# Four tiles of x are turned once and kept, the second half's turns and statistics get fixed steps, and the last z tile's PSUM bank is moved

## Chip, core and metric

One kernel runs on one NeuronCore of a Trainium2 chip. Its engines are TensorE (PE, with its weight loads as PEld), VectorE (DVE), ScalarE (ACT), GpSimd (POOL) and SyncE (SP, which here only issues DMAs). The metric is device time in microseconds (us) of one launch. Three runs of the kernel before gave 1761.16, 1761.31 and 1762.13 us; their median, 1761.31 us, is the number that the change is compared with.

## The reference

Everything is float32; S = 2048 rows, D = 512 columns.

```python
xn = layernorm(x)
# A: 32 heads of 128, keys and values: the last 512 rows of the cache
q = xn @ wq                                   # per head 2048 x 128
s = softmax(q @ k.T * 128 ** -0.5) @ v @ wo
# B: gated MLP with mixing along the rows
z = gelu(xn @ w_in)                           # 2048 x 1376
z1, z2 = z[:, :688], layernorm(z[:, 688:])
g = (z1 * (w_sp @ z2 + b_sp[:, None])) @ w_out
out = x + s * silu(g)
```

## The kernel before, in words

Every product of float32 matrices is made of three matmuls on a high and a low half (`mm3`): ACT casts the high half (`copy`), and DVE or POOL subtracts it from the whole (`rest`, line 59) for the low half. The order of all work is written out by hand; each engine runs its own instructions in the order of the program, and a semaphore holds one back until what it needs is done. SP's DMAs are in that order too.

**Start.** The 16 row tiles of x (128 rows each) are normalised and turned. The first eight lie in `sacc`. `flip` turns one by four transposes through the PE into a PSUM bank, and `ln_flip(i)` splits it into the blocks `X[0]`. There are eight PSUM banks: four in the pool `ps_acc` (name `ps_a`, banks 0 to 3) and four in `ps_step` (`ps_3`, banks 4 to 7). A pool gives out the bank that was released longest ago; whoever writes it first waits for its last reader or writer.

**q by fewer products.** For heads after the first two, q is made in a scheme of seven products in place of eight, which needs sums and differences of tiles p and 4 + p (`T1` to `T4`). The kernel before turns tiles 0 to 3 a second time for them: `t_sums(p)` at steps -3 to 0 of the main loop, with `row_sums` (three operations on DVE) behind it.

**Main loop.** `for t in range(T0, T1)` has 512 numbered steps and some before and behind. Step t holds `score(t)` (scores of one 128-row tile of one head: three matmuls, then DVE's maximum `nm`, then ACT's `prob`), some products of `q_products`, `pv` (three matmuls) for step t - 13, and `outp` (three matmuls, then DVE adds the result to `sacc`, line 592) for step t - 18. DVE also transposes `prob` (`turn`, line 541), a DMA through `p_dram` finishes the turn, and `shares` splits it for `pv`: high on ACT (line 560), low on POOL (`pT_l`). A block of four steps (one head and 512 rows) needs `qT` of its own. q of four blocks is made in a round of 16 steps (`LEAD`, `q_span`, `q_events`): step numbers modulo 16 tell what q does. Its low halves `qT_l` are made on DVE at steps 2, 5 and 9 of 16; the one at step 2 is needed by the score at step 4. `score` and `outp` share the four banks of `ps_step`. With one exception in four, a score waits until DVE has read the `outp` of two steps earlier, and every fourth `outp` (steps 1, 5, 9, 13 of 16) waits for DVE's read of the `outp` just one step earlier.

**Second half of x.** `later_x(p)`, for p = 0 to 3, brings tiles 8 + p and 12 + p during steps 30 to 220: load, statistics on DVE (`tile_stats`: BN_STATS and BN_AGGR; `row_stats`: a TENSOR_SCALAR at line 74, then POOL), normalising on ACT (`apply`), a transposition on DVE (`turn_x`, recorded at line 801), a trip through DRAM (`send`, `fetch`), ACT's reordering (`ordered`), sums on POOL (`sums`) and stores for later. A rule sets its steps: an entry at every 2.4 steps on average, so that they fall where they fall in q's round.

**Behind the loop.** Sixteen tiles of z2 follow (`z_product` into a PSUM bank, `z_gelu`: gelu on ACT and BN_STATS on DVE, `z_norm`). Then the pools close and the mixing begins: `products` writes into the banks of a new pool (`pp2`, line 932), the first of them bank 0. The output projection ends the kernel.

Of the kernel before, what the change touches and what calls it, by code (L numbers as in the profile page):

```python
# [8 lines left out]
F32 = mybir.dt.float32  # L9
# [3 lines left out]
OP = mybir.AluOpType  # L13
# [4 lines left out]
P = 128  # L18
S, D = 2048, 512
H, DH, W = 32, 128, 512  # L20
NT = S // P
NC = D // P
# [18 lines left out]
def mixer_kernel(ctx: ExitStack, tc: tile.TileContext, x, wh, w_in, w_sp, b_sp, w_out, out):  # L41
# [8 lines left out]
    nc = tc.nc  # L50
# [10 lines left out]
    late = []  # L61
# [21 lines left out]
    ps_acc = psum.enter_context(tc.tile_pool(name="ps_acc", bufs=4, space=PSUM))  # L83
# [72 lines left out]
    def block():  # L156
        return x8([P, 2, 2, 512])
# [54 lines left out]
    def flip(t, late=False):  # L212
        ps = ps_acc.tile([P, NC, P], F32, name="ps_a") if late else ps_step.tile([P, NC, P], F32, name="ps_3")
        for c in range(NC):
            nc.tensor.transpose(ps[:, c, :], t[:, c * P:(c + 1) * P], ident)
        return ps

    def ln_flip(i, parts=1):
        n, j = divmod(i, 4)
        if j == 0:  # L220
            for h in range(2):
                X[0][h, n] = block()
        if parts == 1:
            ps = flip(sacc[:, i, :])
        else:
            ps = ps_step.tile([P, NC, P], F32, name="ps_3")
        rests, rest_of = [], []
        for h in range(2):
            if parts > 1:
                for c in (2 * h, 2 * h + 1):  # L230
                    nc.tensor.transpose(ps[:, c, :], sacc[:, i, c * P:(c + 1) * P], ident)
            hi, lo = (quarter(X[0][h, n][:, a], j) for a in range(2))
            nc.scalar.copy(hi, ps[:, 2 * h:2 * h + 2])
            rests.append((lo, ps[:, 2 * h:2 * h + 2], hi))
        if n == 1:
            p2, y = ps.rearrange("p c q -> p (c q)"), sacc[:, i, :]
            nc.scalar.copy(y[:, :256], p2[:, :256])
            rest_of.append((y[:, 256:], p2[:, 256:], y[:, :256]))
        if parts > 1:
            return rests  # L240
        for r in rests:
            rest(nc.vector, *r)
        for r in rest_of:
            nc.vector.tensor_tensor(*r, op=OP.subtract)

    TS = ("T2", "T1", "T3", "T4")

    def row_sums(ps, y, o):

        nc.vector.tensor_tensor(o[:, :256], y[:, :256], ps[:, :256], op=OP.subtract)  # L250
        nc.vector.tensor_tensor(o[:, 256:], ps[:, :256], y[:, 256:], op=OP.add)
        nc.vector.tensor_tensor(y[:, :256], ps[:, 256:], o[:, 256:], op=OP.subtract)

    def t_sums(p):
        if p == 0:
            X[0].update((k, block()) for k in TS)
        row_sums(flip(sacc[:, p, :]).rearrange("p c q -> p (c q)"), sacc[:, 4 + p, :], sacc[:, p, :])

    def t_split(p):
        y, o = sacc[:, 4 + p, :], sacc[:, p, :]  # L260
# [38 lines left out]
    def later_x(p):  # L299

        a, b, key = T8 + p, T8 + 4 + p, 100 * (p + 1)
        t, nb = {}, {}

        def row():
            return xq.tile([P, 512], F32, name="rawx")

        def load():
            for i in (a, b):
                t[i] = row()
                nc.sync.dma_start(t[i], x[i * P:(i + 1) * P, :])  # L310

        def row_stats():
            ln_scale(2, key)
            for k, i in enumerate((a, b)):
                mean, r = rx[key + k]
                nb[i] = tmp[key][:, k:k + 1]
                nc.gpsimd.tensor_scalar(nb[i], mean, r, -1.0, op0=OP.mult, op1=OP.mult)

        def apply(i):
            nc.scalar.activation(t[i], t[i], AF.Identity, bias=nb[i], scale=rx[key + (i == b)][1])  # L320

        def turn_x(i):
            src, t["t", i] = t[i], row()
            late.append((nc.vector.transpose, t["t", i].rearrange("p (a c q) -> p a c q", a=4, q=Q),
                         src.rearrange("p (c a q) -> p a c q", a=4, q=Q)))

        def send(i):
            nc.sync.dma_start(x_turn[p][i == b].rearrange("i r a f -> (i r) (a f)"), t["t", i])

        def fetch(i):  # L330
            t["f", i] = row()
            of = x_turn[p][i == b].rearrange("i r a f -> a r i f")
            for g in range(4):
                nc.sync.dma_start(t["f", i][Q * g:Q * g + Q].rearrange("p (i f) -> p i f", i=4), of[g])

        def ordered(i):
            t[i] = row()
            nc.scalar.copy(t[i].rearrange("p (c i q) -> p i c q", i=4, q=Q), t["f", i].rearrange("p (i c q) -> p i c q", i=4, q=Q))

        def quarters():  # L340
            return [t[i][:, 256 * h:256 * h + 256] for i in (a, b) for h in range(2)]

        def part():
            st = t[0, 1] = xq.tile([P, 512], F32R, name="rawx")
            sl = t[b][:, :256]
            nc.scalar.copy(st[:, :256], sl)
            rest(nc.gpsimd, st[:, 256:], sl, st[:, :256])

        def sums(k):
            b11, b21, b12, b22 = quarters()  # L350
            if k == 0:
                u, v = row(), row()
                t.update({"T1": u[:, :256], "T2": u[:, 256:], "T4": v[:, :256], "T3": v[:, 256:]})
            to, x0, x1, op = (("T1", b12, b11, OP.subtract), ("T3", b22, b12, OP.subtract),
                              ("T2", b22, t["T1"], OP.subtract), ("T4", b21, t["T2"], OP.subtract))[k]
            nc.gpsimd.tensor_tensor(t[to], x0, x1, op=op)

        def store(*ks):
            for k in ks:
                if k in ("a", "b"):  # L360
                    send(a if k == "a" else b)
                elif k in WHOLE:
                    src = t[k] if k in TS else quarters()[2 * k[1] + k[0]]
                    nc.sync.dma_start(xd[1, k][:, :, p * P:(p + 1) * P], halves(src))
                else:
                    nc.sync.dma_start(xd[1, k][:, :, :, p * P:(p + 1) * P],
                                      t[k].bitcast(F32).rearrange("p (a c q) -> p a c q", a=2, q=P))

        seq = [load, None, None, lambda: tile_stats(t[a], key, 0), lambda: tile_stats(t[b], key, 1), row_stats,
               lambda: apply(b),  # L370
               lambda: (turn_x(b), apply(a)),
               lambda: turn_x(a),
               None,
               lambda: fetch(b),
               lambda: fetch(a),
               lambda: ordered(b),
               lambda: ordered(a),
               part,
               lambda: sums(0),
               lambda: sums(1),  # L380
               lambda: sums(2),
               lambda: sums(3)]
        stores = {8: ("b",), 9: ("a",), 14: ((1, 1),), 15: ((0, 0), (1, 0)), 16: ((0, 1), "T1"), 17: ("T3",), 18: ("T2",), 19: ("T4",)}
        return [(f, stores.get(n, ())) for n, f in enumerate(seq + [None])], store
# [23 lines left out]
    def z1_out(i, n, ps):  # L408
        z = zs.tile([P, NB], F32, name="z1")
        nc.scalar.copy(z, ps[:, :NB])  # L410
        nc.scalar.dma_start(z1_dram[:, i, n * NB:(n + 1) * NB], z)

    def z1_piece(i, n, between=lambda: None):
        z1_out(i, n, z1_product(i, n, between))
# [186 lines left out]
    def at(t, f, *args):  # L601
        todo.setdefault(t, []).append((f, args))
# [52 lines left out]
                q_events.setdefault(t0 + done + 2, []).append((q_done, g, k))  # L655

    for p in range(4):
        at(-3 + p, t_sums, p)
        at(-2 + p, t_split, p)
    ends = {}  # L660
    ends.setdefault(-2, []).append((keep_x, (0, 1)))
# [7 lines left out]
    ends.setdefault(16 * (NG - 1) - LEAD + 9, []).append((fetch_x, 1, (0, 1)))  # L669
    for k in ((0, 0), (1, 0)):  # L670
        ends.setdefault(NSTEP + 6, []).append((fetch_x, 0, k))
    n, t = 0, 28
    for p in range(4):
        seq, store = later_x(p)
        for k, (f, ks) in enumerate(seq):
            t = max(t + 2, 30 + 12 * n // 5)
            for key in ks:
                at(t, store, key)
            if f:
                at(t, f)  # L680
            n += 1

    load_x(0, 1)
    load_early(0, [(0, 2)])
# [57 lines left out]
    rest(nc.vector, *lowq)  # L742
    z1_out(0, 1, ps)
    z1_out(1, 1, ps1)
    ln_apply(rows[4], 4)
    ln_apply(rows[5], 5)
    z1_piece(2, 0)
    ln_open(6)
    ln_open(7)
    z1_piece(2, 1)  # L750

    FILL = dict(zip((-7, -6, -5, -4, -3, -2, -1, 0, 1, 8),
                    [(i, 1) for i in range(3, T8)] + [(i, 0) for i in range(4, T8)] + [(3, 0)]))
# [237 lines left out]
    for pos, i in enumerate(ZO):  # L991
        if pos > 2 and pos % 2:
            z_split(pos - 2)
        for n in (2, 3):
            z_product(i, n)
            z_gelu(i, n)
        z_norm(pos)
        z_apply(pos - 1)
        if pos == 5:
            for k in ((0, 1), (1, 1)):  # L1000
                fetch_x(0, k)
        t = pos - NT
        if t in (-6, -4, -3):
            prep((-6, -4, -3).index(t), nc.vector)
        step(t)
# [225 lines left out]
```

## Time and profile before

| what | us |
|---|---|
| median of three runs | 1761.31 |
| the profiled execution, its own time | 1761.58 |
| its span, first to last instruction | 1759.7 |
| start, to the first step of the main loop | 0 to 42.6 |
| main loop | 42.6 to about 1364 |
| z2 of 16 tiles, then mixing from | 1487.2 |
| last matmul | 1755 |

The profile's page gives busy times by engine, the chain of work that ended last and the costliest groups. The waits view adds up who waited for whom. The timeline shows instructions in order of time: its columns are start, duration, engine, line, operation, tiles (out<-in), shape, count, and in brackets the idle time before and what ended it. A matmul's duration includes its way through the array; two matmuls in a row overlap, so the cost of one is the distance between the starts.

### The profile page before, as it was taken

What the parts mean: (1) busy time and instruction counts of PE and PEld (TensorE: products, weight loads), DVE (VectorE), ACT (ScalarE), POOL (GpSimd) and SP (SyncE); (2) the same over time, 40 slices, a digit from 0 to 9 for tenths busy, and PEclk for the clock granted to TensorE, in tenths of its full rate; (3) what the DMA queues carried; (4) which work ended last, traced back from release to release, by engine and by line L of the source; (5) the groups of instructions that cost most, each with busy time, mean ns of one, the idle gap of its engine ahead of it and who ended that gap; (6) DMA issues with size and microseconds to landing.
All of it is one profiled execution on the core that took longest, in us unless ns stands there. A gap on an engine that the chain in (4) does not pass through costs nothing.

```text
span 1759.7 us, 28541 instructions
## 1 busy us (share of the span) xinstructions
PE 1753.1 (100%) x8431; PEld 1503.3 (85%) x8431; DVE 1489.9 (85%) x2458; ACT 1185.8 (67%) x2621; POOL 1239.4 (70%) x1171
## 2 busy tenths in 40 slices
PE   9999999999999999999999999999999999999999
PEld 8888888888888887888888888888888899999997
DVE  6789889899899889988888888888888647887875
ACT  5877777777777777777777777777777546543333
POOL 2888998988988989888888888888888411000032
PEclk9999999999999999999999999999999999999999
DMA  6688888988989989788787777877888652655496
GB/s 204 213 237 260 260 250 242 261 240 244 269 246 253 258 235 273 223 255 223 223 228 219 232 225 220 226 218 225 229 224 255 210 192 86 223 189 176 149 259 204
DMA packets 177468, 398.45 MB, mean 226 GB/s; under 512 B 24480, under 2 KB 58528, under 8 KB 158112
## 3 DMA queue, kind: packets, MB, share of 16 engines
q1 hardware_dynamic: 172704, 390.99, 75.7%
q10 hardware_dynamic: 4608, 5.64, 0.9%
q8 instruction: 66, 1.08, 0.3%
q14 instruction: 90, 0.74, 0.1%
HBM read 231.65 MB, written 164.89 MB: 225 GB/s over the span
## 4 chain that ended last, share of the span: by engine, by line
PE 99%; ACT 0%; DVE 0%; issue 0%; POOL 0%; DVEq 0%; POOLq 0%; ACTq 0%
PE ps_a L503 17%; PE ps L65 13%; PE ps L67 13%; PE ps L66 13%; PE ps L932 11%; PE ps_a L570 7%; PE ps_a L569 7%; PE ps_a L568 7%; PE ps_a L66 2%; PE ps_a L67 2%; PE ps_a L65 2%; PE ps_f L66 1%; PE ps_f L67 1%; PE ps_f L65 1%; PE ps_f L932 1%; PE ps_f L1139 0%
## 5 line engine op out<-in xcount | busy, mean ns | idle before, releaser
L59 POOL TENSOR_TENSOR pT_l<-pL,pT_h 128x512 fp32r<-128x512 f32 x507 | 659.2, 1303 | 170.9 <-ACT pT_h L560 162.6
L532 ACT ACTIVATE prob<-ps,nm 128x512 f32<-128x512 f32 x512 | 353.6, 691 | 340.8 <-DVE nm L530 331.8
L592 DVE SCALAR_TENSOR_TENSOR sacc<-ps,sums,sacc 128x512 f32<-128x512 f32 x496 | 369.3, 745 | 115.0 <-PE ps L67 109.4
L503 PE MATMUL ps_a<-x,x 128*128 128x512 f32 x1266 | 365.5, 389 | 0.0
L541 DVE STREAM_TRANSPOSE pL<-prob 128x512 f32<-128x512 f32 x512 | 358.6, 700 | 0.4 <-ACT prob L532 0.4
L530 DVE TENSOR_REDUCE nm<-ps 128x1 f32<-128x512 f32 x512 | 339.9, 664 | 3.0 <-PE ps L67 2.9
L560 ACT CAST pT_h<-pL 128x512 fp32r<-128x512 f32 x512 | 318.5, 622 | 7.3 <-ACT z L410 4.9
L503 PEld LDWEIGHTS ps_a<-x,x 128*128 128x128 f32 x1266 | 237.7, 188 | 49.3 <-issue 0.2
L59 POOL TENSOR_TENSOR wl<-raw,wh 128x512 fp32r<-128x512 f32 x186 | 241.9, 1300 | 11.0 <-ACT wh L145 11.0
L65 PE MATMUL ps<-wh,qT_h 128*128 128x512 f32 x512 | 200.7, 392 | 0.3 <-DVE sacc L592 0.2
L67 PE MATMUL ps<-wh,qT_l 128*128 128x512 f32 x512 | 200.0, 391 | 0.0
L570 PE MATMUL ps_a<-pT_l,wh 128*128 128x512 f32 x512 | 199.6, 390 | 0.0
L65 PE MATMUL ps<-wh,oT_h 128*128 128x512 f32 x512 | 199.4, 390 | 0.0
L66 PE MATMUL ps<-wl,qT_h 128*128 128x512 f32 x512 | 199.4, 389 | 0.0
L66 PE MATMUL ps<-wl,oT_h 128*128 128x512 f32 x512 | 199.4, 389 | 0.0
L568 PE MATMUL ps_a<-pT_h,wh 128*128 128x512 f32 x512 | 199.4, 389 | 0.0
L569 PE MATMUL ps_a<-pT_h,wl 128*128 128x512 f32 x512 | 199.4, 389 | 0.0
L67 PE MATMUL ps<-wh,oT_l 128*128 128x512 f32 x512 | 199.3, 389 | 0.0
L932 PE MATMUL ps<-b,x 128*128 128x344 f32 x1248 | 191.8, 316 | 0.0
L932 PEld LDWEIGHTS ps<-b,x 128*128 128x128 f32 x1248 | 191.5, 188 | 0.0
L59 POOL TENSOR_TENSOR b<-b 128x512 fp32r<-128x512 f32 x2 | 2.5, 1293 | 189.5 <-DMA x<-x 189.5
L59 POOL TENSOR_TENSOR x<-wq,x 128x256 fp32r<-128x256 f32 x177 | 131.6, 744 | 0.0
(212 smaller groups left out, 3047.7 us busy)
## 6 DMA issues: line engine op xcount, KB each, us to landing
p_dram<-pL SPq DMA_DIRECT2D x128, 1024.0 KB, 4.8
pL<-p_dram SPq DMA_DIRECT2D x256, 192.0 KB, 4.1
raw<-wh SPq DMA_DIRECT2D x188, 256.0 KB, 6.3
pL<-p_dram SPq DMA_DIRECT2D x256, 128.0 KB, 4.1
x<-w_sp SPq DMA_DIRECT2D x24, 1024.0 KB, 5.1
pL<-p_dram SPq DMA_DIRECT2D x256, 64.0 KB, 4.0
wq<-wh SPq DMA_DIRECT2D x60, 256.0 KB, 5.7
z_dram<-z ACTq DMA_DIRECT2D x32, 172.0 KB, 3.0
```

The costliest lines, as they stand in the source:

```text
L59: engine.tensor_tensor(lo, whole, hi.bitcast(F32), op=OP.subtract)
L65: nc.tensor.matmul(ps, lh, rh, start=first, stop=False)
L66: nc.tensor.matmul(ps, lh, rl, start=False, stop=False)
L67: nc.tensor.matmul(ps, ll, rh, start=False, stop=last)
L503: nc.tensor.matmul(qps[g, bank], wt["q", g, k][a][:, c * P:(c + 1) * P], X[g * 2 // H][ORDER[k]][:, b, c], start=first, stop=r == 5, skip_ ...
L530: nc.vector.tensor_reduce(nm, ps, axis=AX.X, op=OP.max, negate=True)
L532: nc.scalar.activation(prob[t], ps, AF.Exp, bias=nm, accum_out=sums[b][:, j:j + 1])
L541: nc.vector.transpose(pL[b][:, :, j * P:j * P + P].rearrange("p a (c q) -> p a c q", q=Q), prob.pop(t).rearrange("p (a c q) -> p a c q", a ...
L568: nc.tensor.matmul(pps[b], vh, ph, start=c == 0, stop=False)
L570: nc.tensor.matmul(pps[b], vh, pl, start=False, stop=c == 3)
L592: nc.vector.scalar_tensor_tensor(at, ps, rs, at, op0=OP.mult, op1=OP.add)
L932: nc.tensor.matmul(ps, a, b, start=k != "P4" and c == 0 and m == 0, stop=c == RP - 1 and m == 2, skip_group_check=True)
```

## The change

The four second turns go. `ln_flip(i)` keeps the bank of each turned tile; for tiles 0 to 3, ACT copies it whole into a row buffer (`keep_whole`), and when tile 4 + p is turned, `row_sums` makes all four differences at once, on DVE, at the end of steps -7 to -4 (pushed on `late`). `t_sums` is gone; `t_blocks` only opens the blocks. Tiles 0 and 1 turn into banks of `ps_acc`.

`later_x(p)` has fixed steps, 28 + 48 p + `WHEN_X[k]`, and its stores 28 + 48 p + `STORE_X[key]`. As 48 is three rounds, each entry falls on the same step of q's round for all p. Both `apply` now stand at one step.

Ahead of the last z product, a bank of `ps_acc` is taken and a memset of one column is written to it, so that the product gets the next bank.

```diff
+    def keep_whole(i):
+        p2, whole[i] = whole[i], xq.tile([P, 512], F32, name="rawx")
+        nc.scalar.copy(whole[i], p2)
...
         if parts == 1:
-            ps = flip(sacc[:, i, :])
+            ps = flip(sacc[:, i, :], i == 1)
         else:
-            ps = ps_step.tile([P, NC, P], F32, name="ps_3")
+            ps = ps_acc.tile([P, NC, P], F32, name="ps_a")
...
         if n == 1:
-            p2, y = ps.rearrange("p c q -> p (c q)"), sacc[:, i, :]
+            y = sacc[:, i, :]
             nc.scalar.copy(y[:, :256], p2[:, :256])
-            rest_of.append((y[:, 256:], p2[:, 256:], y[:, :256]))
+            late.append((row_sums, p2, y, sacc[:, i - 4, :], whole[i - 4]))
+        whole[i] = p2
...
-    def row_sums(ps, y, o):
-
-        nc.vector.tensor_tensor(o[:, :256], y[:, :256], ps[:, :256], op=OP.subtract)
-        nc.vector.tensor_tensor(o[:, 256:], ps[:, :256], y[:, 256:], op=OP.add)
-        nc.vector.tensor_tensor(y[:, :256], ps[:, 256:], o[:, 256:], op=OP.subtract)
-
-    def t_sums(p):
-        if p == 0:
-            X[0].update((k, block()) for k in TS)
-        row_sums(flip(sacc[:, p, :]).rearrange("p c q -> p (c q)"), sacc[:, 4 + p, :], sacc[:, p, :])
+    def row_sums(ps, y, o, x):
+
+        for to, x0, x1 in ((y[:, 256:], ps[:, 256:], y[:, :256]), (o[:, :256], ps[:, :256], x[:, :256]),
+                           (o[:, 256:], ps[:, 256:], o[:, :256]), (y[:, :256], x[:, 256:], o[:, 256:])):
+            nc.vector.tensor_tensor(to, x0, x1, op=OP.subtract)
...
-               lambda: apply(b),
-               lambda: (turn_x(b), apply(a)),
+               lambda: (apply(b), apply(a)),
+               lambda: turn_x(b),
...
-        at(-3 + p, t_sums, p)
+        if p == 0:
+            at(-3, t_blocks)
...
-    n, t = 0, 28
+    STORE_X = {"b": 32, "a": 33, (1, 1): 45, (0, 0): 46, (1, 0): 46, (0, 1): 48, "T1": 48, "T3": 49, "T2": 50, "T4": 51}
+    WHEN_X = (4, 0, 0, 14, 15, 16, 18, 30, 31, 0, 38, 39, 43, 44, 46, 47, 48, 49, 50)
...
-            t = max(t + 2, 30 + 12 * n // 5)
+            t = 28 + 48 * p + (WHEN_X[k] if k < len(WHEN_X) else 0)
             for key in ks:
-                at(t, store, key)
+                at(28 + 48 * p + STORE_X[key], store, key)
...
+    keep_whole(0)
     ln_apply(rows[4], 4)
     ln_apply(rows[5], 5)
-    z1_piece(2, 0)
+    z1_piece(2, 0, lambda: keep_whole(1))
...
-    z1_piece(2, 1)
+    z1_piece(2, 1, lambda: (keep_whole(2), keep_whole(3)))
...
         for n in (2, 3):
+            if (pos, n) == (NT - 1, 3):
+                nc.vector.memset(ps_acc.tile([P, 512], F32, name="ps_a")[:, :1], 0.0)
             z_product(i, n)
```

In numbers, for p = 0 (add 48 for each further p): the statistics move from steps 37 and 39 to 42 and 43, `row_stats` from 42 to 44, the turns from 46 and 49 to 58 and 59, the reordering from 58 and 61 to 71 and 72, POOL's four sums from 66, 68, 70 and 73 to 75, 76, 77 and 78.

What this does on DVE at the four `row_stats` is shown for p = 0, before. The row with rs_t is `row_stats`; `nm` is the maximum of a step's scores, `sacc<-ps` the read of its `outp`.

```order
212 L59 TENSOR_TENSOR qT_l<-ps_a,qT_h 128x512
213 L74 TENSOR_SCALAR rs_t<-mv 128x2
214 L530 TENSOR_REDUCE nm<-ps_1947 128x1
215 L592 SCALAR_TENSOR_TENSOR sacc<-ps_1961,sums,sacc 128x512
216 L541 STREAM_TRANSPOSE pL<-prob 128x4x128
217 L530 TENSOR_REDUCE nm<-ps_1985 128x1
```

And the same place of DVE after the change (steps 42 to 44; the file's lines are some four to six further on):

```order
208 L59 TENSOR_TENSOR qT_l<-ps_a,qT_h 128x512
209 L177 BN_STATS stt<-rawx 128x6
210 L178 BN_AGGR mv<-stt 128x2
211 L534 TENSOR_REDUCE nm<-ps_1926 128x1
212 L596 SCALAR_TENSOR_TENSOR sacc<-ps_1940,sums,sacc 128x512
213 L545 STREAM_TRANSPOSE pL<-prob 128x4x128
214 L177 BN_STATS stt<-rawx 128x6
215 L178 BN_AGGR mv<-stt 128x2
216 L534 TENSOR_REDUCE nm<-ps_1967 128x1
217 L596 SCALAR_TENSOR_TENSOR sacc<-ps_1982,sums,sacc 128x512
218 L545 STREAM_TRANSPOSE pL<-prob 128x4x128
219 L74 TENSOR_SCALAR rs_t<-mv 128x2
```

Both statistics now stand in the two steps just ahead of `row_stats`, and `row_stats` two steps later.

The turn of tile a (step 49, line 801) stood on DVE one step ahead of the `qT_l` of step 50, before:

```order
243 L512 SCALAR_TENSOR_TENSOR ps_a<-ps_a,qs 128x512
244 L541 STREAM_TRANSPOSE pL<-prob 128x4x128
245 L801 STREAM_TRANSPOSE rawx<-rawx 128x512
246 L530 TENSOR_REDUCE nm<-ps_2214 128x1
247 L592 SCALAR_TENSOR_TENSOR sacc<-ps_2228,sums,sacc 128x512
248 L541 STREAM_TRANSPOSE pL<-prob 128x4x128
249 L59 TENSOR_TENSOR qT_l<-ps_a,qT_h 128x512
```

After the change both turns stand at steps 58 and 59 of DVE's order, behind the `qT_l` of step 57 and with none in the steps that follow:

```order
275 L59 TENSOR_TENSOR qT_l<-ps_a,qT_h 128x512
276 L534 TENSOR_REDUCE nm<-ps_2467 128x1
277 L596 SCALAR_TENSOR_TENSOR sacc<-ps_2481,sums,sacc 128x512
278 L545 STREAM_TRANSPOSE pL<-prob 128x4x128
279 L807 STREAM_TRANSPOSE rawx<-rawx 128x512
280 L534 TENSOR_REDUCE nm<-ps_2507 128x1
281 L596 SCALAR_TENSOR_TENSOR sacc<-ps_2522,sums,sacc 128x512
282 L545 STREAM_TRANSPOSE pL<-prob 128x4x128
283 L807 STREAM_TRANSPOSE rawx<-rawx 128x512
```

At the end of z2, DVE's order after the change has the memset between the two BN_STATS of the last tile (before, those two stood together):

```order
2153 L952 TENSOR_TENSOR b<-b 128x2x344 x2
2154 L59 TENSOR_TENSOR b<-b 128x2x344
2155 L853 BN_STATS stz<-b 128x6
2156 L1002 MEMSET ps_a 128x1
2157 L853 BN_STATS stz<-b 128x6
```

On PE, where z2's last product ends and the mixing begins, with the semaphores that a row waits for, first before and then after the change:

```order
6217 L66 MATMUL ps_a<-raw,x_18388 128x344
6218 L67 MATMUL ps_a<-raw,x_18388 128x344
6219 L932 MATMUL ps<-b,x_18590 128x344 [waits Activation_49]
6220 L932 MATMUL ps<-b,x_18590 128x344 [waits DVE_49] x2
6221 L932 MATMUL ps<-b,x_18590 128x344 x10
```

```order
6209 L66 MATMUL ps_a<-raw,x_18376 128x344
6210 L67 MATMUL ps_a<-raw,x_18376 128x344
6211 L938 MATMUL ps<-b,x_18578 128x344 [waits DVE_49]
6212 L938 MATMUL ps<-b,x_18578 128x344 x17
6213 L938 MATMUL ps<-b,x_18664 128x344 [waits Activation_49]
```

The first mixing product goes to bank 0 in both. Before, that bank's last user was a z product of an earlier tile, whose gelu on ACT it waits for. After, it is the bank that the memset wrote, and the count of DVE's semaphore that the matmul waits for is the one that the memset raises.

More of the change, by code (lines that the diff above doesn't have):

```diff
@@ L216, in flip @@
         return ps
+    whole = {}
+    def keep_whole(i):
+        p2, whole[i] = whole[i], xq.tile([P, 512], F32, name="rawx")
+        nc.scalar.copy(whole[i], p2)
     def ln_flip(i, parts=1):
@@ L223, in ln_flip @@
         if parts == 1:
-            ps = flip(sacc[:, i, :])
+            ps = flip(sacc[:, i, :], i == 1)
         else:
-            ps = ps_step.tile([P, NC, P], F32, name="ps_3")
-        rests, rest_of = [], []
+            ps = ps_acc.tile([P, NC, P], F32, name="ps_a")
+        rests = []
         for h in range(2):
@@ L234, in ln_flip @@
             rests.append((lo, ps[:, 2 * h:2 * h + 2], hi))
+        p2 = ps.rearrange("p c q -> p (c q)")
         if n == 1:
-            p2, y = ps.rearrange("p c q -> p (c q)"), sacc[:, i, :]
+            y = sacc[:, i, :]
             nc.scalar.copy(y[:, :256], p2[:, :256])
-            rest_of.append((y[:, 256:], p2[:, 256:], y[:, :256]))
+            late.append((row_sums, p2, y, sacc[:, i - 4, :], whole[i - 4]))
+        whole[i] = p2
         if parts > 1:
@@ L242, in ln_flip, with t_blocks @@
             rest(nc.vector, *r)
-        for r in rest_of:
-            nc.vector.tensor_tensor(*r, op=OP.subtract)
     TS = ("T2", "T1", "T3", "T4")
-    def row_sums(ps, y, o):
-        nc.vector.tensor_tensor(o[:, :256], y[:, :256], ps[:, :256], op=OP.subtract)
-        nc.vector.tensor_tensor(o[:, 256:], ps[:, :256], y[:, 256:], op=OP.add)
-        nc.vector.tensor_tensor(y[:, :256], ps[:, 256:], o[:, 256:], op=OP.subtract)
-    def t_sums(p):
-        if p == 0:
-            X[0].update((k, block()) for k in TS)
-        row_sums(flip(sacc[:, p, :]).rearrange("p c q -> p (c q)"), sacc[:, 4 + p, :], sacc[:, p, :])
+    def row_sums(ps, y, o, x):
+        for to, x0, x1 in ((y[:, 256:], ps[:, 256:], y[:, :256]), (o[:, :256], ps[:, :256], x[:, :256]),
+                           (o[:, 256:], ps[:, 256:], o[:, :256]), (y[:, :256], x[:, 256:], o[:, 256:])):
+            nc.vector.tensor_tensor(to, x0, x1, op=OP.subtract)
+    def t_blocks():
+        X[0].update((k, block()) for k in TS)
     def t_split(p):
@@ L675, in mixer_kernel @@
         for k, (f, ks) in enumerate(seq):
-            t = max(t + 2, 30 + 12 * n // 5)
+            t = 28 + 48 * p + (WHEN_X[k] if k < len(WHEN_X) else 0)
             for key in ks:
-                at(t, store, key)
+                at(28 + 48 * p + STORE_X[key], store, key)
             if f:
                 at(t, f)
-            n += 1
     load_x(0, 1)
```

## The prediction

> **What bounds the kernel now.** I read the page's engine table first, then the waits view for PE, then the starts of PE's matmuls along the timeline.
>
> ```profile
> PE 1753.1 (100%) x8431; PEld 1503.3 (85%) x8431; DVE 1489.9 (85%) x2458; ACT 1185.8 (67%) x2621; POOL 1239.4 (70%) x1171
> ```
>
> PE is busy for 1753.1 of a span of 1759.7 us. So the change can win only what it takes away from PE or what PE waits for, and lose only what makes PE wait. The waits view puts hardly anything there:
>
> ```profile
> PE ps L701 <- POOL ident masks.py:199: 1.3, 1, 1.3
> PE ps L231 <- ACT x L233: 0.5, 1, 0.5
> PE ps L65 <- DVE sacc L592: 0.2, 1, 0.2
> ```
>
> (sum in us, count, longest). This view counts a wait only where the array ran empty. Matmuls overlap, so a short wait shows as a wider distance between two starts. That distance is my measure: 0.23 us between two 512-wide matmuls at full pace (a pair below lasts 0.63, one of them 0.39 to 0.40), 0.16 between two 344-wide ones (33.73 to 33.89).
>
> **The change, part by part.** The sum is made against the profiled execution's 1761.58 us, of which 1.9 lie outside its span; the median shown, 1761.31, is 0.27 lower.
>
> *The four second turns.* One of them on PE:
>
> ```profile
> 33.14 0.60 PE L215 MATMUL ps<-ident,sacc 128*128 128x128 f32 x4
> 33.49 0.40 PE L65 MATMUL ps_a<-wh,x 128*128 128x344 f32 x1
> 33.73 0.32 PE L66 MATMUL ps_a<-wl,x 128*128 128x344 f32 x1
> 33.89 0.32 PE L67 MATMUL ps_a<-wh,x 128*128 128x344 f32 x1
> ```
>
> The four transposes take 0.35 to the next start, and the matmul behind them follows 0.24 before the next instead of 0.16: 0.43 in all. Four times: **-1.7** (-1.77 with the unrounded starts).
>
> *The turns of later_x.* Before, the turn of tile a stands just ahead of the qT_l of step 2 of 16, which the score two steps later needs.
>
> ```profile
> 165.74 0.67 DVE L801 STREAM_TRANSPOSE rawx<-rawx 128x512 f32<-128x512 f32 x1
> 168.15 0.39 PE L67 MATMUL ps<-wh,oT_l 128*128 128x512 f32 x1
> 168.39 0.50 PE L65 MATMUL ps<-wh,qT_h 128*128 128x512 f32 x1
> 168.73 0.40 PE L66 MATMUL ps<-wl,qT_h 128*128 128x512 f32 x1
> 169.12 0.50 PE L67 MATMUL ps<-wh,qT_l 128*128 128x512 f32 x1
> 169.45 0.63 PE L503 MATMUL ps_a<-x,x 128*128 128x512 f32 x2
> ```
>
> From 168.15 to 169.45 four distances make 1.30 where 4 x 0.23 = 0.91 is usual: 0.39 lost. The same happens once in each p, the last time here:
>
> ```profile
> 549.61 0.50 PE L65 MATMUL ps<-wh,qT_h 128*128 128x512 f32 x1
> L801 DVE STREAM_TRANSPOSE rawx<-rawx x8: 664/668/670, 157.1 to 547.0; 128x512 f32<-128x512 f32 x8
> ```
>
> The four lose 0.39 to 0.41 each. After, both turns stand at steps 10 and 11 of 16, where the next qT_l is seven steps away. There each turn delays one step's DVE work by 0.67, and the reads that PE waits for have at least 0.7 left by the trace. I take no loss there: **-1.6**. If the cover were 0.1 short, each turn would cost about 0.2, 1.6 in all.
>
> *row_stats.* Its TENSOR_SCALAR writes a tile of 128 x 2 and should take 0.15; yet:
>
> ```profile
> 144.58 1.27 DVE L74 TENSOR_SCALAR rs_t<-mv 128x2 f32<-128x2 f32 x1
> 144.53 1.29 POOL L59 TENSOR_TENSOR pT_l<-pL,pT_h 128x512 fp32r<-128x512 f32 x1 [1.98 <-ACT pT_h L560]
> 146.89 0.39 PE L67 MATMUL ps<-wh,oT_l 128*128 128x512 f32 x1
> 147.15 0.49 PE L65 MATMUL ps<-wh,qT_h 128*128 128x512 f32 x1
> 147.48 0.39 PE L66 MATMUL ps<-wl,qT_h 128*128 128x512 f32 x1
> ```
>
> It lasts as long as the POOL pass beside it, and ends with it. The score behind it then loses (0.26 - 0.23) + (0.33 - 0.23) = 0.13 to 0.14; four times, **-0.56** when this place is left.
>
> The new place, step 44, is worse in one point: both pairs of statistics now stand in the two steps ahead of it. One pair holds DVE for 131.47 - 130.66 = 0.81:
>
> ```profile
> 130.66 0.68 DVE L177 BATCH_NORM_STATS2 stt<-rawx 128x6 f32<-128x512 f32 x1
> 131.37 0.18 DVE L178 BATCH_NORM_AGGREGATE mv<-stt 128x2 f32<-128x6 f32 x1
> 131.47 0.66 DVE L530 TENSOR_REDUCE nm<-ps 128x1 f32<-128x512 f32 x1
> ```
>
> What stands there otherwise is seen 32 steps later, at steps 74 to 77, where later_x puts nothing on DVE:
>
> ```profile
> 229.50 0.68 DVE L530 TENSOR_REDUCE nm<-ps 128x1 f32<-128x512 f32 x1
> 230.09 0.74 DVE L592 SCALAR_TENSOR_TENSOR sacc<-ps,sums,sacc 128x512 f32<-128x512 f32 x1
> 230.75 0.70 DVE L541 STREAM_TRANSPOSE pL<-prob 128x512 f32<-128x512 f32 x1
> 231.38 0.65 DVE L530 TENSOR_REDUCE nm<-ps 128x1 f32<-128x512 f32 x1
> ```
>
> ```profile
> 230.27 0.69 ACT L532 ACTIVATE prob<-ps,nm 128x512 f32<-128x512 f32 x1 [0.59 <-DVE nm L530]
> 233.38 1.29 POOL L59 TENSOR_TENSOR wl<-raw,wh 128x512 fp32r<-128x512 f32 x1
> 236.57 0.39 PE L65 MATMUL ps<-wh,oT_h 128*128 128x512 f32 x1
> ```
>
> The first pair moves the step's chain back by 0.8: the second pair comes at 231.38 + 0.8 = 232.2, the step behind it runs without a gap (0.8 + 0.6 + 0.65 + 0.65), and the TENSOR_SCALAR reaches DVE at 234.8. ACT and POOL follow the same chain (ACT's prob waits for nm), so POOL's wl pass also moves by 0.8, to about 234.17 to 235.42. The TENSOR_SCALAR is held until its end, and only then nm (to 236.0) and the read of outp (to 236.74) can run. The outp of step 77 (one of those that wait for the read one step before), at 236.57, starts about 236.79, 0.2 late, and the pair behind a wait loses 0.1 more, as above: 0.31 each, **+1.25** for four. The ends: 0 if the TENSOR_SCALAR falls between two POOL passes; if it comes as the pass begins, 0.6 each, 2.4 in all. I take the middle since its place comes from rows.
>
> *The memset.* It is the one new wait of PE. In the rows of order above it stands on DVE between the last tile's two BN_STATS, and the first mixing product waits for it.
>
> ```profile
> 1487.24 13.04 PE L932 MATMUL ps<-b,x 128*128 128x344 f32 x84
> 1491.55 0.93 DVE L847 BATCH_NORM_STATS2 stz<-b 128x6 f32<-128x344 f32 x2
> L697 DVE MEMSET power<- x1: 68/68/68, 0.8 to 0.8; 128x12 f32 x1
> ```
>
> Before, PE goes on at 1487.24 without a gap (1487.24 is one normal distance behind the last z product). DVE is behind by then: the first of the two BN_STATS starts at 1491.55 and the second 0.43 later, at 1491.98. The memset takes the second's place, 0.07 (by the only memset of such a size in a row), and a wait between engines ends about 0.09 after the writer (230.27 - 230.18, the ACT row above). So PE starts at 1492.14 or a little before: 4.9 later, with the loss behind a wait **+5.0**. Its bounds: 0 if nothing really waits; 5.4 if the memset starts only when both BN_STATS are done. From there on PE has no wait to the last matmul, since the mixing products follow each other at 13.04 / 84 = 0.155, so nothing behind takes the loss back. The second BN_STATS ends 0.07 later, which is far less than the 4.9 that PE gives it.
>
> *What is hidden.* ACT's four whole copies stand in a stretch where PE's products lie ahead of ACT:
>
> ```profile
> 18.30 0.45 ACT L410 COPY z<-ps_a 128x344 f32<-128x344 f32 x1 [0.20 <-DMA z_dram<-z]
> 19.14 0.32 PE L65 MATMUL ps_a<-wh,x 128*128 128x344 f32 x1
> ```
>
> The product at 19.14 now takes the bank that this ACT copy frees at 18.75: 0.39 in hand, ahead of the first whole copy. Each of those takes about 0.5 on ACT and fits ACT's idle there; without it, up to 0.5 each, 2 in all; a gain is excluded, since none of PE's work there goes away. DVE's row sums (four of 0.33 instead of three and one) have 0.8 or more in hand. POOL's four sums of 0.74 now stand together at steps 75 to 78, and the next shares' low half comes late by 2.6 of these 3.0:
>
> ```profile
> 242.46 1.31 POOL L59 TENSOR_TENSOR pT_l<-pL,pT_h 128x512 fp32r<-128x512 f32 x1
> 246.77 0.39 PE L570 MATMUL ps_a<-pT_l,wh 128*128 128x512 f32 x1
> ```
>
> It ends at 243.77 and is used at 246.77; 0.4 is left. Both apply at one step and the closer stores move only work of ACT and SP that PE meets many steps later. Nothing for these; from 0 to 2 if POOL's cover is short.
>
> **Sum:** -1.77 - 1.61 - 0.56 + 1.25 + 5.0 = +2.3 on 1761.58, or +2.3 on the median: **1763.6 us**.
>
> [...] At the program's start, PE's first work is slow:
>
> ```profile
> 1.34 5.06 PE L701 MATMUL ps<-ident 128*128 128x128 f32 x24 [1.34 <-POOL ident masks.py:199]
> ```
>
> 24 transposes take 0.21 each, behind 1.34 of idle PE; at 33.14 they take 0.35 / 4 = 0.09. No row of before shows PE idle for over 0.5 after that, so whether 4.9 of idle bring the slow pace back is open. [...]
>
> **The rivals.**
>
> *PE comes back slow (the slower side).* The 4.9 of idle are longer than any in the trace, and at the start PE ran slow from 1.34 until about 5.9, so 4.5 us. If the mixing starts that way, its products take 0.31 instead of 0.155 for that long and 4.5 / 2 = 2.3 are lost: 1765.9. It decides from the idle length at which PE drops, which lies somewhere above 0.5. For it: the slow start. Against it: the start also follows a load of the program, and the last 4.9 come after 1480 us of full work.
>
> *The memset holds nobody.* If the wait ended earlier than I place it, or the last product's new bank also freed PE elsewhere, the 5.0 vanish: 1763.6 - 5.0 = 1758.6, and without the new row_stats stall 1757.4. Against it: the row of order names DVE's count, and DVE's lateness, 4.3 between the end of z on PE and the first BN_STATS, is in the trace.
>
> *POOL's sums come late.* If the 0.4 left is not there, pv stalls in each p by some 0.3 to 0.5, 1 to 2 in all: 1765.1.
>
> **How the numbers follow.** The forecast, with its own range of 1762.3 to 1764.6, gets 0.60; the slow return 0.28, POOL's sums 0.03, the memset that holds nobody 0.09. A measurement of this kernel tells about 0.2% from no change, that is 1757.8 to 1764.8. The forecast lies inside; the slow return (where it costs over 1.2) and POOL's sums outside, together 0.29 with the forecast's upper end and without the slow return's small cases; of the case without the wait, half is below 1757.8. Faster 0.04, same 0.67, slower 0.29. The range leaves out the memset case and the ends of the slow return: 1761.6 to 1766.6.
>
> **What would show it.** PE's timeline: no L215 rows at 27 to 36, no widened starts behind qT_l at step 2 of 16, small ones of 0.3 behind the new TENSOR_SCALAR of about 1 us, and one gap of 4.9 ahead of the first mixing product with a wait put down to DVE's memset. Distances of 0.31 behind it would show the slow return. I am wrong if that gap isn't there, or if waits appear at steps that I took as covered.

## The result, and the profile after

The changed kernel takes 1772.7 us (median of six runs, 1771.72 to 1773.43), the kernel before 1761.66 in the same count of runs: a ratio of 1.0062, interval 1.0049 to 1.0075. It is slower by 11.0 us; forecast was 2.3 more than before, in a range that ended at 1766.6. The profiled execution took 1771.72 us, with a span of 1769.5 (before 1759.7).

The table of engines and then the first rows of PE's waits, after:

```profile
PE 1757.8 (99%) x8415; PEld 1508.6 (85%) x8415; DVE 1488.2 (84%) x2459; ACT 1189.2 (67%) x2625; POOL 1239.5 (70%) x1171
```

```profile
PE ps L938 <- DVE ps_a L1002: 4.8, 1, 4.8
PE ps L706 <- POOL ident masks.py:199: 1.3, 1, 1.3
PE ps L402 <- DVE pT_l L59: 0.5, 1, 0.5
PE ps_a L237 <- ACT x L239: 0.5, 1, 0.5
PE ps_a L67 <- DVE x L59: 0.2, 1, 0.2
```

The span grew by 9.8, but the new wait for the memset is 4.8, and 16 matmuls are gone. PE's busy time is 4.7 more with fewer instructions: its matmuls became slower. Where, is seen by cutting the span at the last z product and at the first mixing product (PE's and DVE's timeline, after):

```profile
1484.59 0.31 PE L67 MATMUL ps_a<-raw,x 128*128 128x344 f32 x1
1489.69 2.65 PE L938 MATMUL ps<-b,x 128*128 128x344 f32 x9 [4.79 <-DVE ps_a L1002]
```

```profile
1489.06 0.95 DVE L853 BATCH_NORM_STATS2 stz<-b 128x6 f32<-128x344 f32 x2
1489.58 0.06 DVE L1002 MEMSET ps_a<- 128x1 f32 x1
```

| part of the span | before | after | difference | forecast |
|---|---|---|---|---|
| to the start of the last z product | 1487.08 | 1484.59 | -2.49 | -2.69 |
| from there to the first mixing product | 0.16 | 5.10 | +4.94 | +4.9 |
| from there to the end | 272.46 | 279.81 | +7.35 | +0.1 |
| sum (span) | 1759.7 | 1769.5 | +9.80 | +2.3 |

The first two rows came close to what was worked out. The third is the miss. Two things make it. The windows view of the changed kernel, just behind the wait (columns: stretch, length, busy time and instructions of PE, PEld, DVE, ACT and POOL, granted clock, DMA share, GB/s):

```profile
1490.00:1494.00 4.00, 4.00 (x17) 4.00 (x16) 3.82 (x9) 2.83 (x4) 1.59 (x2) 0.57 0.00 0
```

The granted clock is 0.57, and only 17 products run in 4 us where 26 are usual: the slow return, a dozen products at 0.287 us ("half pace" below), 1.7 us lost. Within these 4 us the clock is at one half for 3.41 us and full otherwise:

```profile
1490.07:1493.48 3.41, 3.41 (x14) 3.41 (x13) 3.27 (x7) 2.24 (x4) 1.59 (x2) 0.50 0.00 0
```

PE has worked for 3.8 us when the clock returns at 1493.48; in e0_no_memset, below, it has worked for 5.1.

The rest lies at a granted clock of 1.00. PE's windows, 160 us in the middle of the mixing, before and then after (stretch, length, PE's busy time and matmuls, granted clock, DMA share, GB/s):

```profile
1520.00:1680.00 160.00, 160.00 (x1046) 1.00 0.54 181
```

```profile
1520.00:1680.00 160.00, 160.00 (x1016) 1.00 0.52 174
```

30 products fewer in the same time: 160 / 1046 = 153 ns from start to start before, 160 / 1016 = 157.5 after. The single starts give 153.3 and 157.8, without change from 1494 to the end of the mixing at 1703. That is 4.5 ns on each of the 1330 products behind the half pace, 5.9 us (6.0 if all 1344 products of the mixing are wide). With the 1.7 that makes 7.6; the span then ends 0.3 sooner behind the last matmul's start, 4.3 for 4.6. The group of the mixing shows it too, before and after:

```profile
L932 PE MATMUL ps<-b,x 128*128 128x344 f32 x1248 | 191.8, 316 | 0.0
```

```profile
L938 PE MATMUL ps<-b,x 128*128 128x344 f32 x1248 | 199.0, 321 | 4.8 <-DVE ps_a L1002 4.8
```

A mean of 321 for 316 looks like nothing; over 1300 products it is the largest single loss of the change.

### The profile page after: what moved, and what is told of

Read it like the earlier page. It is cut to its first block, busy times and chain, and to the rows that moved or that the text cites. A ratio compares the mean times of both kernels' runs of the same rounds, so it can differ in the third digit from the quotient of the medians.

```text
span 1769.5 us, 28500 instructions
## 1 busy us (share of the span) xinstructions
PE 1757.8 (99%) x8415; PEld 1508.6 (85%) x8415; DVE 1488.2 (84%) x2459; ACT 1189.2 (67%) x2625; POOL 1239.5 (70%) x1171
## 4 chain that ended last, share of the span: by engine, by line
PE 97%; DVE 2%; ACT 0%; DMA 0%; issue 0%; POOL 0%; SPq 0%; ACTq 0%; DVEq 0%; POOLq 0%
PE ps_a L507 16%; PE ps L65 13%; PE ps L67 13%; PE ps L66 13%; PE ps L938 11%; PE ps_a L574 6%; PE ps_a L573 6%; PE ps_a L572 6%; PE ps_a L67 2%; PE ps_a L65 2%; PE ps_a L66 2%; PE ps_f L66 1%; PE ps_f L67 1%; PE ps_f L65 1%; PE ps_f L938 1%; PE ps_f L1147 0%
## 5 line engine op out<-in xcount | busy, mean ns | idle before, releaser
L938 PE MATMUL ps<-b,x 128*128 128x344 f32 x1248 | 199.0, 321 | 4.8 <-DVE ps_a L1002 4.8
L938 PEld LDWEIGHTS ps<-b,x 128*128 128x128 f32 x1248 | 198.5, 189 | 5.1 <-DVE ps_a L1002 5.1
```

The costliest lines, as they stand in the source:

```text
L938: nc.tensor.matmul(ps, a, b, start=k != "P4" and c == 0 and m == 0, stop=c == RP - 1 and m == 2, skip_group_check=True)
```

## The experiments

The wide distances are put down to one of three causes. Theory "wait": any wait of PE ahead of the mixing leaves these wider distances behind. Rival "cold": they are what is left of a long idle and its half pace. Rival "bank": they come of the moved banks or of other engines' traffic.

**The memset at other places of DVE's order** (e1_early, e2_wait_1, e3_wait_3). Banks and operations stay; the last z products are written earlier in the program (PE's order is the same), with the memset between them, so that DVE reaches it sooner. The edit shown is e1_early's; the other two move the last tile alone, to later places.

```diff
+    def last_tiles():
+        for i, n in ((ZO[-2], 2), (ZO[-2], 3), (ZO[-1], 2), (ZO[-1], 3)):
+            if (i, n) == (ZO[-1], 3):
+                nc.vector.memset(ps_acc.tile([P, 512], F32, name="ps_a")[:, :1], 0.0)
+            z_product(i, n)
...
         for n in (2, 3):
-            if (pos, n) == (NT - 1, 3):
-                nc.vector.memset(ps_acc.tile([P, 512], F32, name="ps_a")[:, :1], 0.0)
-            z_product(i, n)
+            if pos < NT - 2:
+                z_product(i, n)
             z_gelu(i, n)
+        if pos == NT - 3:
+            last_tiles()
```

> The memset is issued on DVE right behind the BN_STATS of the third last z tile (about 1483.0), so that it is done before PE ends z at 1484.7; banks and instructions stay those of the changed kernel. Its profiled execution took 1771.72 us; if the wait of 4.95, the half pace behind it (1.71) and the wider distances of the 1240 mixing products (157.8 ns instead of 153.3, 5.56) all hang on PE's wait, all three go: 1759.5 us, distances 153.3. If the wider distances come from the moved banks or from other engines' traffic (rival), only the wait and the half pace go: 1765.1 us, distances 157.8.

> The memset behind the BN_STATS of the last tile but one (about 1485.6): PE waits 0.9 to 1.0. If any wait at this place leaves the wide distances behind (theory 'wait'): no half pace, distances 157.8 for all the mixing, 1759.5 + 1.1 + 5.6 = 1766.2 us. If the wide distances are what is left of a long idle and its half pace (theory 'cold'): 153.3 and 1760.6 us.

> The memset behind the differences of that step (about 1487.5): PE waits 2.8 to 2.9. Theory 'wait': 157.8 and 1759.5 + 3.0 + 5.6 = 1768.1 us, half pace or not. Theory 'cold': 1762.5 us with 153.3 if 2.8 us of idle are too short for the half pace; with half pace and 157.8, up to 1770.

| run | PE waits | us | ratio to before, interval | distance in the mixing |
|---|---|---|---|---|
| e1_early | none | 1759.64 | 0.9989 (0.9980 to 0.9998) | 153.3 ns |
| e2_wait_1 | 0.8 | 1766.70 | 1.0029 (1.0018 to 1.0040) | 157.8 ns |
| e3_wait_3 | 2.7 | 1769.67 | 1.0047 (1.0033 to 1.0060) | 157.8 ns |

PE's windows over the same 160 us, e1_early and then e2_wait_1, and the latter's wait:

```profile
1520.00:1680.00 160.00, 160.00 (x1045) 1.00 0.55 179
```

```profile
1520.00:1680.00 160.00, 160.00 (x1016) 1.00 0.51 169
```

```profile
1485.04 0.31 PE L67 MATMUL ps_a<-raw,x 128*128 128x344 f32 x1
1486.19 13.99 PE L938 MATMUL ps<-b,x 128*128 128x344 f32 x87 [0.83 <-DVE ps_a L999]
```

Theory "wait" stands, and both rivals fall: e1_early has the moved banks and none of the wide distances, and e2_wait_1 has them without half pace (its first 87 products take 0.16 each at once). One small wait costs 7.06 us here: 1.0 for itself, 0.1 for the pair behind it, and 1344 x 4.5 ns = 6.0. In e3_wait_3 the profiled execution (1768.66) fits the theory, without half pace; the other three took 0.8 to 2.1 more. There is no trace of those, so what they lost stays open; the granted clock over the whole run is 0.999 in them and 1.000 in the profiled one, which would fit a stretch at half pace, but before has runs of 0.999 too.

**No memset** (e0_no_memset). The tile is taken and not written; then it doesn't count as a user, and the last z product goes into bank 0.

```diff
-                nc.vector.memset(ps_acc.tile([P, 512], F32, name="ps_a")[:, :1], 0.0)
+                ps_acc.tile([P, 512], F32, name="ps_a")
```

> The dummy tile is taken but not written, so there is no memset and the last z product goes into bank 0; the first mixing product then waits for ACT's gelu of that product (about 1489.0) instead of for DVE: an idle of 4.2. If what is behind the wait hangs on PE's idle alone, whoever ends it: half pace of 1 to 2 us and 157.8 again, 1759.5 + 4.3 + 1.5 + 5.6 = 1770.9 us. If it hangs on the memset or the moved bank: 1763.8 us, 153.3.

1771.3 us (ratio 1.0049, 1.0035 to 1.0063), 157.8 ns, and 16 products at half pace (PE's wait, and then the window in which the clock is at one half, 6.8 us):

```profile
1489.53 10.78 PE L938 MATMUL ps<-b,x 128*128 128x344 f32 x52 [4.08 <-ACT b L852]
```

```profile
1487.84:1494.66 6.82, 5.13 (x18) 5.13 (x19) 5.88 (x12) 5.63 (x10) 1.59 (x2) 0.50 0.02 7
```

So it is no matter of DVE or of the memset: ACT ends this wait, and all that follows is the same. The run also shows what the moved bank does here: without it, PE waits 4.1 for ACT's gelu; with it, 4.8 for DVE. Both engines are behind at this place. One of its four runs took 1765.48, some 6 less than the others, as much as the wide distances cost; it has no trace.

**What ends the wide distances** (e5_burst). In the main loop of before, most products behind a wait are 2 to 9 ns wider, for 3 to 10 matmuls of 512 columns, and then no more. So matmuls of 512 columns were put into the mixing of e2_wait_1:

```diff
+        if n == 2:
+            wide = HL[MOVING[k], 0]
+            for m in range(15):
+                nc.tensor.matmul(bank[r, k].rearrange("p (c f) -> p c f", c=2), ops[n][:, 0, 0],
+                                 wide[:, 0, :, :256], start=True, stop=True, skip_group_check=True)
```

> e2_wait_1 with 15 extra 512-wide products, whose results are overwritten, ahead of the third bank of the mixing (36 products behind the wait). In the trace of before, the wide distances behind each wait in the main loop last for 4 to 10 products of 512 columns and then end. If products of 512 columns end them here too: + 15 x 0.23 = 3.4 and - 1204 x 4.5 ns = 5.4, so 1766.7 - 2.0 = 1764.7 us, 153.3 behind the extra products. If the state lasts as long as the mixing does, whatever runs in it: 1766.7 + 3.5 = 1770.2 us, 157.8.

1767.92 us. The program passes this place twice, so 30 extra products ran, not 15 (the second 15 also overwrite what the bank's first 18 products had summed). By that count, 30 x 0.227 = 6.8 more and 1308 x 4.5 ns = 5.9 less than e2_wait_1: 1767.6. The timeline around the first 15, and the window:

```profile
1491.00 0.95 PE L943 MATMUL ps<-b,x 128*128 128x344 f32 x5
1491.79 3.60 PE L937 MATMUL ps<-b,x 128*128 128x512 f32 x15
1495.23 2.00 PE L943 MATMUL ps<-b,x 128*128 128x344 f32 x12
```

```profile
1520.00:1680.00 160.00, 160.00 (x1045) 1.00 0.53 176
```

The first nine of the 15 follow each other at 224 to 236 ns, the others at 226 to 227, and behind them the mixing runs at 153.3. So the wide distances are a state that a wait starts, that nine matmuls of 512 columns end, and that 1300 of 344 columns don't.

**PE kept at work while it waits** (e6_fill). 24 extra products behind the last z product of the changed kernel:

```diff
+            if (pos, n) == (NT - 1, 3):
+                fill = ps_step.tile([P, 512], F32, name="ps_3")
+                for m in range(24):
+                    nc.tensor.matmul(fill[:, :NB], x_op(i, 0, 0), wt[("w", n), 0][0][:, :NB], start=True, stop=True)
```

> The changed kernel with 24 extra 344-wide products into a spare bank behind the last z product, so that PE works for 3.7 of the 4.95 us of its wait; the wait for the memset stays, about 1.2 are left of it. If the half pace comes of PE's idle time: it is gone, the wide distances stay (a wait of 0.9 to 1.0 left them in e2_wait_1): 1759.6 + 5.0 + 5.6 = 1770.2 us with little spread between runs. If it comes of the wait's end on DVE or the new bank: as the changed kernel, 1771.7 to 1773.4 us.

1770.92 us (1770.81 to 1771.31). 1.12 are left of the wait, the wide distances stay, and the clock stays at 1.00 (last row):

```profile
1485.43 3.84 PE L1007 MATMUL ps<-wh,x 128*128 128x344 f32 x24
1490.39 9.89 PE L938 MATMUL ps<-b,x 128*128 128x344 f32 x61 [1.12 <-DVE ps_a L1002]
```

```profile
1490.00:1494.00 4.00, 3.61 (x23) 3.62 (x24) 3.83 (x10) 2.83 (x5) 1.59 (x2) 1.00 0.01 4
```

The half pace comes of PE's idle time (a clock of 0.50 behind an idle of 4.8 in the changed kernel, 1.00 behind 1.12 here) and is a loss of its own; the wide distances need only a wait.

**The fixed steps of later_x alone** (e8_schedule), on the kernel before (the diff's part on `later_x`, `WHEN_X` and `STORE_X`).

> The kernel before with the fixed steps of later_x alone: by the terms of the sum -1.61 (turns) - 0.56 (row_stats left) + 1.29 (row_stats at step 44) = -0.88, so 1760.6 us. If the fixed steps cost more than they save (POOL's four sums together, both apply at one step): 1761.5 us or more, with new waits at steps 72 to 80 of the trace.

1761.06 us, beside 1761.94 for before: -0.88, as the three terms have it, though the interval of the ratio (0.9995, 0.9987 to 1.0004) holds no change too. The traces show it more sharply. The scores of steps 20 and 300, first in before and then in e8_schedule:

```profile
83.88 0.39 PE L65 MATMUL ps<-wh,qT_h 128*128 128x512 f32 x1
825.45 0.39 PE L65 MATMUL ps<-wh,qT_h 128*128 128x512 f32 x1
```

```profile
84.50 0.39 PE L65 MATMUL ps<-wh,qT_h 128*128 128x512 f32 x1
825.19 0.39 PE L65 MATMUL ps<-wh,qT_h 128*128 128x512 f32 x1
```

Between them lie 741.57 us before and 740.69 with the fixed steps: -0.88. The start, which is the same in both programs, took 0.62 longer in this execution of e8_schedule.

**What holds DVE at row_stats.** The changed kernel at the first of them, DVE, POOL and PE:

```profile
148.36 0.68 DVE L74 TENSOR_SCALAR rs_t<-mv 128x2 f32<-128x2 f32 x1
```

```profile
147.72 1.30 POOL L59 TENSOR_TENSOR wl<-raw,wh 128x512 fp32r<-128x512 f32 x1
```

```profile
149.92 0.39 PE L574 MATMUL ps_a<-pT_l,wh 128*128 128x512 f32 x1
150.35 0.50 PE L65 MATMUL ps<-wh,oT_h 128*128 128x512 f32 x1
150.69 0.39 PE L66 MATMUL ps<-wl,oT_h 128*128 128x512 f32 x1
```

The TENSOR_SCALAR ends with POOL's wl pass, and outp starts 0.20 late and loses 0.11 behind it, as forecast. Three kernels, from e1_early, move this small addition: to a TENSOR_TENSOR on DVE (e7_tt), to POOL (e9_pool), to ACT (e10_act). The line that does it in each:

```diff
...
+            nc.vector.tensor_tensor(v, mv[key][:, :2, 1], eps, op=OP.add)
...
```

```diff
...
-            ln_scale(2, key)
+            ln_scale(2, key, nc.gpsimd)
```

```diff
...
+            nc.scalar.activation(v, mv[key][:, :2, 1], AF.Identity, bias=eps[:, :1], scale=1.0)
...
```

> e1_early with the TENSOR_SCALAR of row_stats in later_x replaced by a TENSOR_TENSOR with a tile that holds the constant, at the same place on DVE. If the TENSOR_SCALAR is held by POOL's pass as read in the trace, and the TENSOR_TENSOR is not: it takes about 0.1 and the four stalls of 0.32 go, 1759.64 - 1.29 = 1758.35 us. If the stalls come from the two pairs of statistics ahead of it alone: 1759.6 us.

> e1_early with the small addition of row_stats in later_x (a tile of 128 x 2) on POOL instead of DVE. In e7_tt a TENSOR_TENSOR at that place on DVE lasted 0.68 and ended with POOL's pass just like the TENSOR_SCALAR, so that run could not tell. If holding this small operation is the stall: DVE goes on to nm 0.6 earlier, the four waits of 0.2 and their 0.11 behind go, 1759.65 - 1.28 = 1758.4 us, the wide starts at 150, 277, 404 and 531 gone. If the two pairs of statistics alone make the stall: 1759.6 us, stalls as before; if POOL's extra 0.3 makes its shares late: up to 1760.7.

> As e9_pool, but the small addition of row_stats in later_x is made by ACT (an activation of 128 x 2 with the constant as bias). In e9_pool the stalls of 0.32 at 150, 277, 404 and 531 went, and POOL's low half of the shares came 0.19 late five us later, in each p (0.78 in all). If DVE's held operation was the stall, and POOL's extra work the new one, neither is there now: 1759.65 - 1.28 = 1758.4 us. If one small operation costs its price wherever it stands (ACT late with prob): 1759.3 us, with new wide starts within 6 us of 150.

e7_tt: 1759.67 us, nothing gained. The expectation that a TENSOR_TENSOR isn't held was wrong (the row has the least, median and greatest ns of the four):

```profile
L319 DVE TENSOR_TENSOR rs_t<-mv,power x4: 672/679/680, 148.5 to 529.1; 128x2 f32<-128x2 f32 x4
```

e9_pool: 1759.33 us. The four stalls at 150 to 531 are gone, and four of 0.18 to 0.23 stand at 155 to 536, where pv waits for POOL's pT_l: 0.78 of the 1.25 came back. The first of them:

```profile
155.53 0.39 PE L573 MATMUL ps_a<-pT_h,wl 128*128 128x512 f32 x1
155.83 0.50 PE L574 MATMUL ps_a<-pT_l,wh 128*128 128x512 f32 x1
156.16 0.40 PE L65 MATMUL ps<-wh,oT_h 128*128 128x512 f32 x1
```

e10_act: 1758.71 us, with neither the one nor the other in its trace. The place of the first stall in it:

```profile
150.26 0.39 PE L579 MATMUL ps_a<-pT_l,wh 128*128 128x512 f32 x1
150.49 0.39 PE L65 MATMUL ps<-wh,oT_h 128*128 128x512 f32 x1
150.72 0.39 PE L66 MATMUL ps<-wl,oT_h 128*128 128x512 f32 x1
```

Its ratio to before is 0.9982 (0.9973 to 0.9991): with the memset early, this is the fastest version of the study, 3.0 us below before. So the held operation was the stall, and the two pairs of statistics only bring it to that place.

## Why the prediction was wrong

- **The memset, +5.0: the step that failed.** Its wait was right (4.94), and so were its place and the engine that is late. What failed is the sentence that the mixing products "follow each other at 13.04 / 84 = 0.155" behind it, so that nothing follows the wait: in each traced run with a wait at this place they follow at 157.8 ns (in e5_burst only up to its wide products), some 6 us in all. The row that shows it was in the prediction: 0.16 between the 344-wide products at 33.73 and 33.89, beside 0.155 in the mixing. Both were called a normal distance. In the start of before the narrow products run at 157 to 158 from 15 us to the main loop, where matmuls of 512 columns follow each other.
- **The slow return, a rival at 0.28.** It came, and in this execution costs 1.7 (forecast 2.3; its 0.31 for each product over 4.5 us was the author's estimate, which no run shows: here a dozen took 0.287, within 3.4 us at half clock). Without the wide distances the time would have been about 1766.7, near the 1765.9 of that case. The idle of 4.1 (e0_no_memset) and 4.8 brought it; none shows in the profiled execution with 2.7. The profiled execution of the changed kernel has it and is the quickest of the six, so the other five most likely had it too, against the 0.28 that the forecast gave it. Four of the six took 1772.4 to 1773.4 at a granted clock of 0.998 over the whole run, the other two 1771.7 and 1771.9 at 0.999; the profiled execution of e0_no_memset, with 6.8 us at half clock, has 0.998. So those four may have been at half clock for about as long, which no trace of theirs shows.
- **The turns, -1.61, and row_stats, -0.56 and +1.25: right.** The stalls of before are gone, four new ones of 0.31 to 0.32 stand where they were forecast, and e8_schedule alone gives -0.88 where the terms give -0.92. From the score of step 20 to that of step 300 the changed kernel gains 0.90.
- **The four second turns, -1.77, with what hides the rest at nothing: half right.** e1_early, which has all of the change but the wait, gains 1.87 and not 2.69; with -0.88 for the schedule, some 1.0 is left for the turns. In the ten traces with the new start, the score of step 20 comes 0.9 to 1.6 sooner than in before, but e8_schedule, with before's start, has it 0.6 later than before; so the size is known to some tenths only. A term was missed in "what is hidden": DVE's row sums. The last of the four differences reads only rows in SBUF and ran beside a POOL pass, in all ten traces; in the changed kernel:

```profile
27.00 0.43 DVE L258 TENSOR_TENSOR sacc<-rawx,sacc 128x256 f32<-128x256 f32 x1
29.91 1.10 DVE L258 TENSOR_TENSOR sacc<-rawx,sacc 128x256 f32<-128x256 f32 x1
```

```profile
29.45 1.29 POOL L59 TENSOR_TENSOR wl<-raw,wh 128x512 fp32r<-128x512 f32 x1 [5.75 <-DVE sacc L258]
```

```profile
31.40 0.42 PE L67 MATMUL ps_a<-wh,x 128*128 128x344 f32 x1 [0.17 <-DVE x L59]
```

  Its likes take 0.42 to 0.43 (27.00 and two later ones, beside an idle POOL); the product that waits behind it loses 0.44. The 0.8 in hand had not reckoned with that. Smaller waits at 24 to 25, 0.1 to 0.4 by execution, may be the rest. No run takes these terms apart: they are read from the traces alone.
- **POOL's sums, the early copies, the stores:** no new wait at steps 72 to 80, but for one distance 0.05 wider at 245 in e10_act.

## What to carry to other kernels

Measure the distance between matmul starts stage by stage, and ask what sets it, before calling it PE's pace: here, with PE busy for 99% of the span, 4.5 ns on each of 1330 products, 5.9 us, outweighed every wait of the page (the longest 4.8). Ahead of a long run of narrow products a wait of 0.8 us may cost seven (7.06 in e2_wait_1, with 1344 products of 344 columns behind it); clear it by doing the work that ends it earlier (e1_early has no wait there), or let wide products that are due anyway come first behind it (no run has that; extra ones cost more than they saved in e5_burst, 1767.92 for 1766.70). A small operation on an engine that is behind is as late as that engine's backlog, not as long as its duration (the memset lasts 0.06, and PE waited 4.8 for it).

## What the hardware showed that was not expected

- Two lasting paces of PE at a granted clock of 1.00: 153.3 or 157.8 ns for 344 columns, about 227 or 231 for 512. A wait of PE nearly always leaves the slower one behind (behind 119 of the 131 waits of the twelve traces after 43 us that widened a distance by over 0.02 us), down to waits that cost 0.05 us. Ten or so products of 512 columns end it, often fewer; 1300 of 344 didn't. Now and then a wait leaves the faster one: behind the same wait at 31 us, the changed kernel goes on at 153 and e6_fill at 158. What in the chip holds the two apart no run here shows.
- A TENSOR_TENSOR of 128 x 2 on DVE is held by POOL's pass just like a TENSOR_SCALAR (0.68 each; in the changed kernel the TENSOR_SCALAR of 128 x 2 at 22.75, beside no such pass, takes 0.17), while BN_AGGR and RECIPROCAL beside such passes keep their 0.18 and 0.13. The row sum at 29.91, with both inputs in SBUF, is held too (1.10 for 0.43); the one at 29.45, beside the same pass and with one input in PSUM, keeps its 0.42. What sets the held operations apart no run shows.
